# Moving the second stage of the later transforms to other places of a scheduled spectral mixture-of-experts kernel

## The chip, the cores and the metric

The kernel runs on one core of a Trainium2 chip. The metric is the time of one execution on the device in microseconds; the median of several runs counts.

## The reference

For each of 8 batches of 3072 tokens with 256 channels, the reference takes a real FFT along the tokens, multiplies by a complex filter, transforms back, and sends the result through two feed-forward layers:

```python
Y = np.fft.rfft(x, axis=1) * (filt_r + 1j * filt_i)
x = np.fft.irfft(Y, n=3072, axis=1)
xk = mu_k * x + (1 - mu_k) * x_prev
xr = mu_r * x + (1 - mu_r) * x_prev
v = np.maximum(xk @ w_k, 0) ** 2 @ w_v
x = sigmoid(xr @ w_r) * v
h = max(x @ w1, x @ w2, x @ w3)
out = h @ w_out
```

`x_prev` is `x` one token earlier. `w_k` is 256 x 1024, `w_v` 1024 x 256, `w_r` 256 x 256, `w1` to `w3` are 256 x 768, `w_out` is 768 x 256.

## The kernel before, in words

**Work.** A batch is one transform, and its 3072 tokens make 8 chunks of 384. Chunks are numbered through, 64 in all, and two of them make a pair. `kv(i)` (line 1367) is the first layer of chunk i: `r_mm`, then eight f-steps, each with six matmuls of `k_mm` (1204) and, from the fourth f-step on, six of `v_mm` (1217) for the f-step three back; the last three `v_mm` and `x2` are a tail that `mixed` (1457) sets between the units of what follows. `combos` (1236) makes sums of a pair's results. `second(p)` (1398) is the second layer of pair p: nine blocks of seven products (`block`, 1264), block k = 3 fq + j for weight j of the three and feature group fq; the last three products of a block run beside the next block. `out` (1311) takes the maximum over j, and at j = 2 splits it into two parts (`hh`, on ACT and POOL). `o_mm` (1335) multiplies these by `w_out`; it becomes due at k = 3, 6 and 9, with two calls to a block from k = 4 on, and what is left goes into the `kv` that follows. One `po` bank serves two calls of `o_mm` and stays open over all three groups. The main loop runs kv(2p+2), second(p), kv(2p+3) for one p after the other.

**The transform** (`fft`, 816) of a later batch runs inside this work, in pieces that hang at places: `put(place, fn)` (1465) files a piece, and `at_place` (1363) issues it when the loop comes to ("kv", i, f) or ("second", p, k). The first stage is 17 `a_step`s; their results go to DRAM (`s1a`, `s1b`; ACT copies them out of PSUM as `ao` and issues the write). The second stage has six steps u = 0 to 5. `b_load(u)` (894) loads matrices (`wbc`), the first stage's rows (`xb`) and two filter tiles (`filt`), five DMAs on SP's queue; `b_load(0)` is issued by the last `a_step`, `b_load(u+1)` by step u. `b_mm(u)` (908) multiplies into two PSUM banks (`pb`). `b_filt(u, z)` (914) multiplies bank z by the complex filter: ACT's two multiplications by a sign into `v`, DVE's three multiplications into `filt`, then POOL. `c_mm(u)` (933) transforms back from the two `yz` tiles into two banks (`pc`), one place later; `c_out` (939) copies them out on ACT (`co`) and writes them to `s2`, from which `y_load` (1151) and `y_mm` (1164) make the chunks. PSUM has eight banks, all under one tag (`pm`).

Transform b (1 to 7) is laid out at lines 1468 to 1489. For b from 2 on, with i = 8(b-1) and p = 4(b-1)-1, the last `a_step` is at ("kv", i+1, 7), and the second stage's seven places start at ("kv", i+2, 1), which comes right after kv(i+1).

**The order.** All calls after the opening are recorded by `Order` (220). PE's order is the order of the calls. For ACT, DVE, POOL and SP `play` (489) simulates the program with a cost for each instruction (`cost`, 292): `takes_ns` until its result is there, `holds` until its engine is free. Each engine takes, of the instructions that are ready, the one that is due first (`plan`, 329; `run`, 340). Calls are then issued in the order of the simulated starts. `use` (252) notes what an instruction has to wait for: here, writes before reads, and reads before writes. The waits in the program itself are set afterwards, from the issued order.

Of the kernel before, what the change touches and what calls it, by code (L numbers as in the profile page):

```python
# [32 lines left out]
NU4 = NG // 4  # L33
# [186 lines left out]
class Order:  # L220
# [31 lines left out]
    def use(self, o, ap, write):  # L252
        if isinstance(ap, Ref):
            name, dram = ap.tile.name, ap.tile.space == "DRAM"
        else:
            name, dram = ap.tensor.name, ap.space == bass.MemoryType.DRAM
        t = self.tiles.get(name)
        if t is not None:
            if not t.users and not t.early and t.order is not None:
                o.takes.append(t)  # L260
            if t not in o.takes and t.order is not None:
                o.needs.append(t.name)
            t.users.append(o.k)
        lo, hi, p0, p1 = self.box(ap)
        kept = []
        for e in self.seen.get(name, ()):
            k, w, a, b, c, d = e
            meet = a < hi and lo < b and c < p1 and p0 < d
            both = o.engine == "PE" and self.calls[k].engine == "PE" if k < o.k else True
            if meet and not both and (w or write) and not (dram and write):  # L270
                o.before[k] = True
            if not (write and not dram and lo <= a and b <= hi and p0 <= c and d <= p1):
                kept.append(e)
        kept.append((o.k, write, lo, hi, p0, p1))
        self.seen[name] = kept
# [16 lines left out]
    def cost(self, o, out, ins, k):  # L292
        n = int(np.prod(out.shape[1:]))
        psum = any(isinstance(v, Ref) and v.tile.space == "PSUM" for v in ins)
        e = o.engine
        o.shared = False
        o.quarter = False
        if "dma" in o.what:
            o.kind = "dma"
            o.holds = self.ISSUE[e]  # L300
            o.bytes = 4 * int(np.prod(out.shape))
            o.takes_ns = 0
            return
        o.kind = "op"
        if e == "PE":
            if k.get("tile_position") is not None:
                o.quarter = True
                o.holds, o.takes_ns = n // 2, 595
            elif k["lhsT"].dtype == F32R:
                o.holds = 4 + n * 0.4455 - (2 if n == 384 else 0)  # L310
                o.takes_ns = o.holds + 163
            else:
                o.holds = max(212, 8 + n * 1.667)
                o.takes_ns = o.holds + 165
        elif e == "ACT":
            o.takes_ns = 186 + n * 0.8 if psum else 175 + n * 0.89
            if n < 256:
                o.takes_ns = 330
        elif e == "DVE":
            both = len([v for v in ins if np.prod(v.shape[1:]) > 1]) > 1  # L320
            o.takes_ns = 150 + n * 1.065 if psum or both else 65 + n * 0.7
            o.shared = not psum
        else:
            o.takes_ns = 190 + n * 2.16 if len(ins) > 1 else 200 + n * 1.96
            o.shared = True
        if e != "PE":
            o.holds = o.takes_ns - self.OVERLAP[e]

    def plan(self, times):
        t, last = {}, 0.0  # L330
# [283 lines left out]
def tile_spectral_moe(ctx: ExitStack, tc, x, xr, xz, filt, ones, wa, wa1, wi, wbc, wb1, wc1, filt1, filt0, mu, w_k, w_v, w_r, w1, w2, w3, w_out, out):  # L614
    nc = tc.nc
# [42 lines left out]
    sg_s = cpool.tile([NK, 1], F32, name="sg_s")  # L658
# [157 lines left out]
    def fft(b):  # L816
# [48 lines left out]
        def quarters(o, of, whole=False):  # L865

            for k in range(1 if whole else 2):
                for y in (1, 0):
                    for x in range(2):
                        w, d = of(y, x, k)  # L870
                        to = o[y][x * H : x * H + H] if whole else o[y][x * H : x * H + H, k]
                        mm(to, w, d, k == 0, True, True, (y * H, x * H))
# [35 lines left out]
        def b_mm(u):  # L908
            w, f, t = st.pop(("b", u))
            p = [ps.tile([NK, 2, C], F32, tag="pm", name="pb") for _ in range(2)]  # L910
            quarters(p, lambda y, x, k: (w[y * H : y * H + H, 0, x, k], t[y * H : y * H + H, 2 * x + k]))
            st["f", u] = w, f, p, []

        def b_filt(u, z):
            w, f, p, y = st["f", u]
            fr, fi, q = f[z][:, 0], f[z][:, 1], p[z]
            v = fp.tile([NK, 2, C], F32, tag="flo", name="v", bufs=3)
            a, e = slice(0, NM), slice(NM, H)
            lo, hi = slice(H, H + NM), slice(H + NM, NK)
            nc.scalar.mul(v[lo], q[hi], sg_s[hi])  # L920
            nc.scalar.mul(v[hi], q[lo], sg_s[lo])
            nc.vector.scalar_tensor_tensor(fi[a], q[e], -1.0, fi[a], ALU.mult, ALU.mult)
            nc.vector.tensor_tensor(fi[e], q[a], fi[e], ALU.mult)
            nc.vector.tensor_tensor(fr, q, fr, ALU.mult)
            nc.gpsimd.tensor_tensor(fi[H:], v[H:], fi[H:], ALU.mult)
            yz = fp.tile([NK, 2, C], F32, tag="fin", name="yz")
            nc.gpsimd.tensor_tensor(yz, fr, fi, ALU.add)
            y.append(yz)
            if z:
                del st["f", u]  # L930
                st["c", u] = w, y

        def c_mm(u):
            w, t = st.pop(("c", u))
            p = [ps.tile([NK, 2, C], F32, tag="pm", name="pc") for _ in range(2)]
            quarters(p, lambda y, x, k: (w[y * H : y * H + H, 1, x, k], t[x][y * H : y * H + H, k]))
            st["o", u] = p

        def c_out(u, y):
            p = st["o", u][y]  # L940
            o = fp.tile([NK, 2, C], F32, tag="fo", name="co")
            nc.scalar.copy(o, p)
            g = 4 * u + 2 * y
            nc.scalar.dma_start(s2.rearrange("h m r g c -> (h m r) g c")[:, g : g + 2, :], o)

        def bc_step(u):
            if u < NU4:
                b_mm(u)
            if u:
                c_mm(u - 1)  # L950
            if u + 1 < NU4:
                b_load(u + 1)
            for z in range(2):
                if u < NU4:
                    b_filt(u, z)
            for z in range(2):
                if u:
                    c_out(u - 1, z)

        return a_step, bc_step  # L960

    def fft_first(pp, jobs, more):

# [182 lines left out]
    nc = order.nc  # L1146
# [301 lines left out]
    for _ in range(8):  # L1448

        p = ps.tile([P, NT], F32, tag="pm", name="pz")  # L1450
# [12 lines left out]
    steps = {}  # L1463

    def put(place, *fns):
        plan.setdefault(place, []).extend(fns)

    def transform(b):
        a_step, bc_step = fft(b)
        places, counts, bc = steps[b]  # L1470
        u = 0
        for place, n in zip(places, counts):
            for _ in range(n):
                put(place, lambda u=u: a_step(u))
                u += 1
        for u, place in enumerate(bc):
            put(place, lambda u=u: bc_step(u))

    for b in range(1, B):
        i, p = NCH * (b - 1), NCH // 2 * (b - 1) - 1  # L1480
        if b == 1:
            places = [("second", 0, k) for k in range(9)]
            bc = [("kv", 4, 1), ("kv", 4, 6), ("second", 1, 3), ("kv", 5, 7), ("kv", 6, 3), ("second", 2, 1), ("second", 2, 5)]
            counts = [2] * 8 + [1]
        else:
            places = [("kv", i, f) for f in (0, 2, 4, 6)] + [("second", p, k) for k in (4, 5, 6, 7, 8)] + [("kv", i + 1, f) for f in range(8)]
            bc = [("kv", i + 2, 1), ("second", p + 1, 3), ("kv", i + 3, 2), ("kv", i + 3, 7), ("kv", i + 4, 3), ("second", p + 2, 3), ("kv", i + 5, 3)]
            counts = [1] * 17
        steps[b] = places, counts, bc

    units = list(kv0)
    tail = []
    for i in (1, 2, 3):
        u, t = kv(i)
# [3 lines left out]
        tail = t  # L1498
    before2 = len(units)
    units.append(lambda: transform(1))  # L1500
    s, left = second(0)
    units += mixed(tail, s, 2)
    cm = lambda p: [lambda: combos(p)]
    tail = cm(1)
    for p in range(1, NPAIR):
        i = 2 * p + 2
        if i < NTOT:
# [3 lines left out]
            u, t = kv(i, left if p == 1 else ())  # L1511
# [5 lines left out]
        if i + 1 < NTOT:  # L1517
            end = i + 2 == NTOT
            u, t = kv(i + 1, () if end else left)
# [63 lines left out]
```

## Time and profile before

| | us |
|---|---|
| median of 3 runs | 3172.13 |
| lowest and highest | 3170.17, 3172.26 |
| profiled execution | 3172.82 |
| its span | 3171.1 |
| PE busy in it | 3066.8 (97%) |
| DVE, ACT, POOL busy | 1927.7, 1904.8, 1671.8 |

The span runs from the first profiled instruction to the last. Busy time is the union of an engine's instructions; matmuls are pipelined, so a busy PE is not one at its peak. A wait is the idle time of an engine before an instruction, booked on what came last.

### The profile page before, as it was taken

To read this page: it belongs to the slowest core of one execution; us is meant where nothing else is said; L and a number is where in the kernel's file an instruction comes from. 1 tells how busy PE (TensorE), PEld (TensorE's weight loads), DVE (VectorE), ACT (ScalarE), POOL (GpSimd) and SP (SyncE) were. 2 spreads that over 40 slices of the span, in tenths; PEclk is the share of its full clock that TensorE was granted. 3 is DMA by queue.
4 is the path that set the end of the run, shared out by engine and by line. 5 is a ranking of instruction groups with operands and counts; after the bars stand their busy time and mean duration, and the time that the engine had idled before them with its cause. 6 is when DMAs were issued, how large, how long until landed. Compare 5 with 4: busy or idle time off the path is not lost.

```text
span 3171.1 us, 56339 instructions
## 1 busy us (share of the span) xinstructions
PE 3066.8 (97%) x19816; PEld 2929.2 (92%) x19816; DVE 1927.7 (61%) x3061; ACT 1904.8 (60%) x3901; POOL 1671.8 (53%) x1416
## 2 busy tenths in 40 slices
PE   8899999999999999999999999999999999999998
PEld 5898999889998899899998999989999899999998
DVE  6886566566556665466655666556666565555554
ACT  6556656565655655566555665656555566555554
POOL 5435654575545655456445655457544465454543
PEclk9899999999999999999999999999999999999999
DMA  7788577766577765767656776576766765555554
GB/s 239 225 297 270 187 246 227 226 215 222 162 234 214 252 203 169 221 211 254 196 183 202 233 227 214 183 220 218 229 194 213 230 203 158 169 168 163 165 167 121
DMA packets 385192, 660.22 MB, mean 208 GB/s; under 512 B 41472, under 2 KB 150176, under 8 KB 384624
## 3 DMA queue, kind: packets, MB, share of 16 engines
q1 hardware_dynamic: 319584, 581.94, 59.5%
q10 hardware_dynamic: 64720, 72.52, 6.6%
q8 instruction: 159, 2.61, 0.4%
q0 software_dynamic: 608, 2.16, 0.2%
q14 instruction: 121, 0.99, 0.1%
HBM read 573.75 MB, written 82.71 MB: 207 GB/s over the span
## 4 chain that ended last, share of the span: by engine, by line
PE 87%; DMA 4%; ACT 3%; DVE 3%; POOL 2%; issue 1%; ACTq 0%; SPq 0%; POOLq 0%; DVEq 0%
PE pb L241 20%; PE pk L241 16%; PE pv L241 15%; PE po L241 12%; PE pe L241 9%; PE pa L241 6%; PE pr L241 4%; PE py L241 4%; ACT v L241 1%; DVE filt L241 1%; POOL hh L241 1%; PE ps L241 1%; DMA xb<-s1a 1%; DMA wci<-in_wc 1%; PE pc L241 1%
## 5 line engine op out<-in xcount | busy, mean ns | idle before, releaser
L241 POOL TENSOR_TENSOR hh<-m,hh 128x384 fp32r<-128x384 f32 x384 | 435.4, 1152 | 747.2 <-ACT hh L241 667.8
L241 PE MATMUL pb<-x,ws 128*128 128x384 f32 x3456 | 751.5, 339 | 23.0 <-ACT pa L241 17.1
L241 POOL TENSOR_TENSOR klo<-kr,khi 128x384 fp32r<-128x384 f32 x492 | 537.7, 1101 | 343.7 <-ACT khi L241 311.5
L241 PEld LDWEIGHTS pb<-x,ws 128*128 128x128 f32 x3456 | 600.2, 188 | 57.1 <-ACT pa L241 30.4
L241 DVE SCALAR_TENSOR_TENSOR kr<-pk,kr 128x384 f32<-128x384 f32 x512 | 281.9, 553 | 412.8 <-ACT kr L241 404.3
L241 PE MATMUL pv<-khi,ws 128*128 128x384 f32 x2048 | 525.7, 337 | 2.4 <-DVE filt L241 2.4
L241 PE MATMUL po<-wo_hi,hh 128*128 128x256 f32 x2304 | 500.4, 282 | 13.2 <-POOL hh L241 12.7
L241 PEld LDWEIGHTS po<-wo_hi,hh 128*128 128x128 f32 x2304 | 391.3, 189 | 16.2 <-POOL hh L241 15.5
L241 PE MATMUL pe<-x,ws 128*128 128x384 f32 x1728 | 395.2, 336 | 1.9 <-ACT ao L241 1.9
L241 ACT ACTIVATE kr<-pk 128x384 f32<-128x384 f32 x512 | 251.1, 490 | 207.2 <-PE pk L241 121.7
L241 PEld LDWEIGHTS pv<-khi,ws 128*128 128x128 f32 x2048 | 366.9, 189 | 8.7 <-DMA xb<-s1a 4.5
L241 PE MATMUL pk<-xh,wk_hi 128*128 128x384 f32 x1024 | 352.5, 344 | 5.5 <-DVE kr L241 2.9
L241 PE MATMUL pv<-klo,ws 128*128 128x384 f32 x1024 | 344.5, 336 | 1.4 <-POOL klo L241 1.4
L241 PE MATMUL pk<-xl,wk_hi 128*128 128x384 f32 x1024 | 344.6, 337 | 0.1
L241 PE MATMUL pk<-xh,wk_lo 128*128 128x384 f32 x1024 | 344.2, 336 | 0.0
L241 ACT CAST khi<-kr 128x384 fp32r<-128x384 f32 x512 | 261.3, 513 | 131.6 <-DVE kr L241 113.3
L241 POOL TENSOR_TENSOR xl<-xm,xh 128x768 fp32r<-128x768 f32 x126 | 239.7, 1916 | 185.7 <-ACT xh L241 183.2
L241 PE MATMUL po<-wo_lo,hh 128*128 128x256 f32 x1152 | 324.2, 281 | 0.0
L241 ACT CAST hh<-m 128x384 fp32r<-128x384 f32 x384 | 187.9, 514 | 195.4 <-DVE m L241 193.5
L241 DVE TENSOR_TENSOR m<-sc,m 128x384 f32<-128x384 f32 x384 | 297.4, 775 | 5.8
L241 PEld LDWEIGHTS pe<-x,ws 128*128 128x128 f32 x1728 | 295.8, 188 | 5.1 <-ACT ao L241 4.4
L241 ACT COPY u<-pb 128x384 f32<-128x384 f32 x288 | 138.1, 479 | 175.5 <-PE pb L241 173.3
(135 smaller groups left out, 5537.8 us busy)
## 6 DMA issues: line engine op xcount, KB each, us to landing
ws<-wud SPq DMA_DIRECT2D x864, 256.0 KB, 3.3
ws<-wvd SPq DMA_DIRECT2D x512, 256.0 KB, 3.1
filt<-in_filt SPq DMA_DIRECT2D x84, 512.0 KB, 4.7
ws<-wud SPq DMA_DIRECT2D x288, 128.0 KB, 3.3
xz<-in_xz SPq DMA_DIRECT2D x56, 512.0 KB, 5.8
cin<-s SPq DMA_DIRECT2D x128, 192.0 KB, 3.2
out_dram<-osb ACTq DMA_DIRECT2D x192, 128.0 KB, 3.1
xr<-in_xr SPq DMA_DIRECT2D x56, 384.0 KB, 5.0
```

The lines of the kernel that those rows point to most:

```text
L241: o = SimpleNamespace(engine=engine, call=lambda: call(*map(real, a), **{n: real(v) for n, v in k.items()}), what=call.__name__, k=len(sel ...
```

## The change

Four things change. (1) For transforms 2 to 7 the seven places of the second stage are others: a new function `spread` gives them. `bc_step` is parted into `b_step` and `c_step`; `c_step(u)` still hangs at the place of `b_step(u+1)`, and is now issued ahead of it. Transform 1 keeps its places. (2) In `b_filt` the second half (z = 1) issues ACT's two multiplications after DVE's three, the first half before them, as up to now. (3) The costs of ACT and DVE instructions are changed by some per cent, the sign multiplications get a cost of their own, and `holds` is longer for outputs on fewer than 128 partitions and for outputs in PSUM. (4) `use` makes a read of a PSUM tile wait, in the simulated order, for earlier reads of the same tile by another engine.

```diff
--- before.py
+++ after.py
@@ -263,9 +263,12 @@
             t.users.append(o.k)
         lo, hi, p0, p1 = self.box(ap)
         kept = []
+        psum = isinstance(ap, Ref) and ap.tile.space == "PSUM"
         for e in self.seen.get(name, ()):
             k, w, a, b, c, d = e
             meet = a < hi and lo < b and c < p1 and p0 < d
+            if not (w or write) and psum and k < o.k and self.calls[k].engine != o.engine:
+                o.before[k] = True
             both = o.engine == "PE" and self.calls[k].engine == "PE" if k < o.k else True
             if meet and not both and (w or write) and not (dram and write):
                 o.before[k] = True
@@ -313,18 +316,23 @@
                 o.holds = max(212, 8 + n * 1.667)
                 o.takes_ns = o.holds + 165
         elif e == "ACT":
-            o.takes_ns = 186 + n * 0.8 if psum else 175 + n * 0.89
+            o.takes_ns = 176 + n * 0.8 if psum else 175 + n * 0.88
             if n < 256:
-                o.takes_ns = 330
+                o.takes_ns = 342
+            if o.what == "mul":
+                o.takes_ns = 681 if psum else 614
         elif e == "DVE":
             both = len([v for v in ins if np.prod(v.shape[1:]) > 1]) > 1
-            o.takes_ns = 150 + n * 1.065 if psum or both else 65 + n * 0.7
+            o.takes_ns = 147 + n * 1.065 if psum or both else 65 + n * 0.7
             o.shared = not psum
         else:
             o.takes_ns = 190 + n * 2.16 if len(ins) > 1 else 200 + n * 1.96
             o.shared = True
         if e != "PE":
-            o.holds = o.takes_ns - self.OVERLAP[e]
+            part = out.shape[0] < 128
+            o.holds = o.takes_ns - self.OVERLAP[e] if not part else o.takes_ns + 40
+            if isinstance(out, Ref) and out.tile.space == "PSUM":
+                o.holds = o.takes_ns + 20
 
     def plan(self, times):
         t, last = {}, 0.0
@@ -917,11 +925,17 @@
             v = fp.tile([NK, 2, C], F32, tag="flo", name="v", bufs=3)
             a, e = slice(0, NM), slice(NM, H)
             lo, hi = slice(H, H + NM), slice(H + NM, NK)
-            nc.scalar.mul(v[lo], q[hi], sg_s[hi])
-            nc.scalar.mul(v[hi], q[lo], sg_s[lo])
+            def swap():
+                nc.scalar.mul(v[lo], q[hi], sg_s[hi])
+                nc.scalar.mul(v[hi], q[lo], sg_s[lo])
+
+            if not z:
+                swap()
             nc.vector.scalar_tensor_tensor(fi[a], q[e], -1.0, fi[a], ALU.mult, ALU.mult)
             nc.vector.tensor_tensor(fi[e], q[a], fi[e], ALU.mult)
             nc.vector.tensor_tensor(fr, q, fr, ALU.mult)
+            if z:
+                swap()
             nc.gpsimd.tensor_tensor(fi[H:], v[H:], fi[H:], ALU.mult)
             yz = fp.tile([NK, 2, C], F32, tag="fin", name="yz")
             nc.gpsimd.tensor_tensor(yz, fr, fi, ALU.add)
@@ -943,21 +957,19 @@
             g = 4 * u + 2 * y
             nc.scalar.dma_start(s2.rearrange("h m r g c -> (h m r) g c")[:, g : g + 2, :], o)
 
-        def bc_step(u):
-            if u < NU4:
-                b_mm(u)
-            if u:
-                c_mm(u - 1)
+        def b_step(u):
+            b_mm(u)
             if u + 1 < NU4:
                 b_load(u + 1)
             for z in range(2):
-                if u < NU4:
-                    b_filt(u, z)
+                b_filt(u, z)
+
+        def c_step(u):
+            c_mm(u)
             for z in range(2):
-                if u:
-                    c_out(u - 1, z)
-
-        return a_step, bc_step
+                c_out(u, z)
+
+        return a_step, b_step, c_step
 
     def fft_first(pp, jobs, more):
 
@@ -1466,27 +1478,33 @@
         plan.setdefault(place, []).extend(fns)
 
     def transform(b):
-        a_step, bc_step = fft(b)
-        places, counts, bc = steps[b]
+        a_step, b_step, c_step = fft(b)
+        places, counts, bp, cp = steps[b]
         u = 0
         for place, n in zip(places, counts):
             for _ in range(n):
                 put(place, lambda u=u: a_step(u))
                 u += 1
-        for u, place in enumerate(bc):
-            put(place, lambda u=u: bc_step(u))
+        for u in range(NU4):
+            put(bp[u], lambda u=u: b_step(u))
+            put(cp[u], lambda u=u: c_step(u))
+
+    def spread(i, p):
+        bc = [("kv", i + 2, 7), ("second", p + 1, 5), ("kv", i + 3, 1), ("kv", i + 3, 6), ("kv", i + 4, 3), ("second", p + 2, 4), ("kv", i + 5, 2)]
+        return bc[:-1], bc[1:]
 
     for b in range(1, B):
         i, p = NCH * (b - 1), NCH // 2 * (b - 1) - 1
         if b == 1:
             places = [("second", 0, k) for k in range(9)]
             bc = [("kv", 4, 1), ("kv", 4, 6), ("second", 1, 3), ("kv", 5, 7), ("kv", 6, 3), ("second", 2, 1), ("second", 2, 5)]
+            bp, cp = bc[:-1], bc[1:]
             counts = [2] * 8 + [1]
         else:
             places = [("kv", i, f) for f in (0, 2, 4, 6)] + [("second", p, k) for k in (4, 5, 6, 7, 8)] + [("kv", i + 1, f) for f in range(8)]
-            bc = [("kv", i + 2, 1), ("second", p + 1, 3), ("kv", i + 3, 2), ("kv", i + 3, 7), ("kv", i + 4, 3), ("second", p + 2, 3), ("kv", i + 5, 3)]
+            bp, cp = spread(i, p)
             counts = [1] * 17
-        steps[b] = places, counts, bc
+        steps[b] = places, counts, bp, cp
 
     units = list(kv0)
     tail = []
```

## Rows read from the trace of the kernel before

**Rows 1.** The page: busy us, share of the span and instructions of each engine.

```profile
PE 3066.8 (97%) x19816; PEld 2929.2 (92%) x19816; DVE 1927.7 (61%) x3061; ACT 1904.8 (60%) x3901; POOL 1671.8 (53%) x1416
```

**Rows 2.** PE's waits from 560 to 2640 us: us in total, times, longest us.

```profile
PE pb L241 <- DMA xb<-s1a: 30.3, 6, 5.9
PE pb L241 <- ACT pa L241: 12.5, 11, 1.5
PE po L241 <- POOL hh L241: 10.3, 12, 0.9
PE pk L241 <- DVE kr L241: 2.7, 6, 0.5
PE pv L241 <- DVE filt L241: 2.4, 6, 0.4
PE pb L241 <- DMA xb<-s1b: 0.8, 1, 0.8
PE pb L241 <- ACT u L241: 0.5, 3, 0.2
```

**Rows 3.** The chain of waits, 1326 to 1342 us: start us, us, what.

```profile
1331.11 3.56 DMA s1a<-ao
...
1335.32 4.41 DMA xb<-s1a
...
1339.86 2.10 PE pb L241 x16
```

**Rows 4.** Windows after the six stops (first, last, sum): busy us, then PEclk, DMA share, GB/s.

```profile
573.00:577.30 4.30, 4.19 (x23) 3.38 (x24) 1.45 (x3) 2.02 (x3) 0.56 (x1) 0.50 0.84 188
...
2488.70:2492.20 3.50, 3.50 (x21) 2.74 (x22) 0.80 (x2) 1.36 (x2) 0.00 (x0) 0.51 0.84 199
sum 24.60, PE 24.45 PEld 19.75 DVE 8.15 ACT 10.98 POOL 2.94; mean PE 4.07 PEld 3.29 DVE 1.36 ACT 1.83 POOL 0.49
```

**Rows 5.** Timeline of PE, 1333 to 1348 us: start us, us, instruction, count.

```profile
1344.29 0.52 PE L241 MATMUL pk<-xl,wk_hi 128*128 128x384 f32 x1
1344.61 0.52 PE L241 MATMUL pk<-xh,wk_lo 128*128 128x384 f32 x1
...
1346.53 0.33 PE L241 MATMUL pk<-xh,wk_lo 128*128 128x384 f32 x1
1346.70 0.51 PE L241 MATMUL pv<-khi,ws 128*128 128x384 f32 x2
...
1347.74 0.34 PE L241 MATMUL pk<-xh,wk_hi 128*128 128x384 f32 x1
```

**Rows 6.** PE's waits from 320 to 560 us, the largest.

```profile
PE pb L241 <- DMA ws<-wud: 1.8, 1, 1.8
```

**Rows 7.** Timeline of all engines around ("second", p+2, 3), 1083 to 1097 us, with [idle before].

```profile
1083.31 1.09 PE L241 MATMUL pb<-xb,wbc 64*64 64x256 f32 x16
...
1085.92 0.68 DVE L241 TENSOR_TENSOR filt<-pb,filt 32x512 f32<-32x512 f32 x1 [0.75 <-ACT v L241]
...
1086.63 1.38 ACT L241 ACTIVATE v<-pb,sg_s 32x512 f32<-32x512 f32 x2 [0.75 <-DVE filt L241]
...
1088.04 0.46 ACT L241 COPY pa<-pb 128x384 f32<-128x384 f32 x1
...
1088.56 0.79 PE L241 MATMUL pb<-x,ws 128*128 128x384 f32 x3 [1.53 <-ACT pa L241]
...
1094.45 0.68 DVE L241 TENSOR_TENSOR filt<-pb,filt 128x512 f32<-128x512 f32 x1
...
1095.39 0.39 PE L241 MATMUL po<-wo_hi,hh 128*128 128x256 f32 x1 [0.86 <-POOL hh L241]
```

**Rows 8.** Timeline of PE behind ("kv", i+3, 2), 1030 to 1040 us.

```profile
1036.36 0.59 PE L241 MATMUL pv<-khi,ws 128*128 128x384 f32 x2 [0.40 <-DVE filt L241]
...
1037.57 0.44 PE L241 MATMUL pk<-xh,wk_hi 128*128 128x384 f32 x1 [0.45 <-DVE kr L241]
```

**Rows 9.** Window of rows 7: busy us of PE, PEld, DVE, ACT, POOL, PEclk, DMA share, GB/s.

```profile
1083.00:1097.00 14.00, 11.46 (x86) 9.61 (x85) 10.52 (x19) 9.08 (x19) 9.29 (x8) 1.00 0.76 251
```

## The prediction

> **What bounds the kernel now.** I read the busy shares first: TensorE (PE) is busy 97% of the span and every other engine is far below [rows 1], so only what PE waits for, or what slows its matmuls, can move the end. Then I read PE's waits in the stretch that holds transforms 2 to 7, the ones whose places move [rows 2]. Their sum there is 59.5 us, and the largest item, 30.3 us in six pieces, is the first second-stage matmul of each transform waiting for its own load `xb`. The chain of waits around one of them shows why [rows 3]: the write of the first stage's last rows takes 3.56 us, the load that reads them back 4.41 us, and PE starts `pb` as soon as the load has landed. The order asks for `xb` two f-steps after the first stage ends, and a write and a read of HBM do not fit in there.
>
> The windows behind those six stops [rows 4] show a second cost: the granted clock is 0.50 to 0.53, the 1.2 GHz level, after PE has stood still for five or six microseconds. There, two matmuls of 384 columns start 0.32 us apart, and 0.17 us once the clock is back [rows 5]. The other waits of [rows 2] are short and belong to the later places: ACT `pa` and POOL `hh` in the two places in `second`, DVE `filt` and `kr` in the first place of `kv` after it.
>
> **The change part by part.** No matmul, vector operation or DMA is added or removed, so this is a sum of waits.
>
> *First place, six f-steps later.* One f-step issues six matmuls for `k_mm`, and from the third on six for `v_mm`; six take 1.04 us, from 1346.70 to 1347.74 [rows 5]. From ("kv", i+2, 1) to ("kv", i+2, 7) there are six `k_mm`, five `v_mm` and the last `v_mm` of the tail: 12 x 1.04 = 12.5 us. The longest wait of the six is 5.9 us [rows 2], so 6.6 us of cover remain, which a slower write or load would have to eat first. I take all six waits as gone: 30.3 us. A wait is counted from the end of the matmul before it, but back-to-back matmuls overlap (0.33 us long, started 0.17 us apart [rows 5]), so each removed wait brings 0.16 us more: 1.0 us. Bounds: 31.3 and 0. With the step move the five loads that `b_load(1)` puts on SP's queue and both filters' work. SP's loads of streamed weights run eight pieces ahead; the one case where PE did wait for such a piece cost 1.8 us [rows 6], so six transforms could lose at most 10 us by it. I take 0, because in transforms 2 to 7 no such wait appears though the same loads already pass there [rows 2].
>
> *The clock behind these stops.* The six low windows add up to 24.6 us [rows 4]. At half rate they hold the work of 12.3 us, so 12 us come back if no stop of that length takes their place. Bounds: 12 and 0. The Trainium skill, in "TensorE: Matmul & The Clock Gate" (Part 1), advises against fitting the ramp, since it is under 1% of a typical span; by that advice the 12 us would be left out and the forecast would read 3120 us. The rows have the clock at half for these windows, so they decide.
>
> *Places in* `second`, *from k = 3 to 5 and from 3 to 4.* What happens at k = 3 is in the timeline [rows 7]. ACT and DVE read the same `pb` banks in turns: DVE `filt` waits 0.75 us for ACT `v`, ACT `v` 0.75 us for DVE `filt`. ACT's copy `pa`, which PE needs next, stands in ACT's queue behind two such multiplications and starts at 1088.04; PE loses 1.53 us. Later the same filter work delays `hh`, which the first `o_mm` needs in the block after; PE loses 0.86 us. k = 3 is the one block where the block before ends a group (j = 2, four `hh` splits) and `o_mm` wants them at once in k = 4. At k = 5 the next `o_mm` of a new group is two blocks away, at k = 4 the `hh` that is due has been split already. So I take the `hh` waits as gone: 10.3 us, and 12 x 0.16 = 1.9 us, in all 12.2. The `pa` waits (12.5 + 0.8 us booked on `xb<-s1b`, and 1.9 us for 12 overlaps, 15.2 in all) have another cause, a 0.68 us multiplication ahead of a copy on ACT, and that can happen in any block. The new order knows that the two engines take turns at a bank, and the alternation of the second filter half lets DVE start one half while ACT does the other, so the ping-pong should shrink; I take half, 7.6 us. Bounds: all 15.2, and none.
>
> *Places in* `kv`. ("kv", i+3, 2) becomes 1, which puts one `k_mm` and one `o_mm` more between the step and the first `v_mm` that wants two banks. The waits are 2.4 us for DVE `filt`, which holds a bank, and 2.7 us for `kr`, queued behind it, in twelve pieces [rows 2, 8], with overlaps 7.0 us. But `y_mm` now follows the step instead of preceding it and asks for two banks and for ACT. I take half, 3.5 us. Bounds: 7.0 and, if `y_mm` waits as long as `v_mm` did, 0. The other three places move by at most one step and show no wait now.
>
> *c before b on PE, the alternation, the costs.* In one place PE now runs `c_mm(u-1)` ahead of `b_mm(u)`: the same 32 matmuls, 0. It lets ACT empty the two `pc` banks while PE works on `pb`. The alternation alone moves two 0.68 us operations per half on ACT behind DVE's; nothing on PE's path waits for them unless a bank is short: 0. The new costs and the read-after-read rule reorder all queues. Where PE has no wait, there is slack and I take 0; for new short waits at the twelve places in `second` I subtract 3 us, a quarter of a microsecond each (estimate: less than half of one 0.68 us multiplication), with 0 and -18 us (each place as bad as the 1.53 us of [rows 7]) as bounds. The opening and transform 1, whose places stay, I take as 0, with 4 us either way (estimate: two waits like that of [rows 6]).
>
> **The sum.** 31.3 + 12 + 12.2 + 7.6 + 3.5 - 3 = 63.6 us. The profiled execution took 3172.82 us, 1.7 us beyond its span of 3171.1; its forecast is 3109. The median of the three runs lies 0.7 us lower: **3108 us**. A change under 0.2%, some 6 us, could not be told from none.
>
> **Rivals.** (1) *The filter's waits move with it.* The `xb` waits and the clock come back, but the 34.5 us of short waits (28.7 and 36 overlaps) stay at the new places: 3172.1 - 43.3 = 3129 us. For it: ACT's 0.68 us multiplications stay as they are, and the new rule serialises every two reads of one PSUM tile by two engines. The Trainium skill ("PSUM — Partial Sum Buffer", PSUM bank collisions raise a hardware error) keeps two engines apart per bank and 32-partition quadrant only, which would make part of these turns unnecessary; [rows 7] show the waits between 32-partition pieces all the same, since the program waits by tile. Against it: the `hh` wait needs k = 3. (2) *Everything goes*, all 34.5 us: 31.3 + 12 + 34.5 = 78 us, 3094 us. (3) *The chain only moves.* ACT's copies, the write and the load are ordered by when they are due; due 12.5 us later, they could be put behind other work by as much, and PE would still wait about 5 us. Then only the 23.3 - 3 of the places come: 3152 us. Against it: an operation that is ready goes as soon as its queue is free, and ACT is busy only 60% [rows 1]. (4) *Slower: banks run out at k = 5.* One `po` bank is open there and none at k = 3; with two of `pc`, two of `pb`, the running block's and the late block's, eight may not do. The filter keeps its `pb` banks from 1083.31 until 1095.13 [rows 7], 11.8 us; if PE has to wait for them after some 4 us of other matmuls, that is 8 us at 12 places, 94 us, and at half clock afterwards some 2 us each [rows 4], 24 us more: 3172 + 118 - 43 = 3247 us. It decides from 43/12 = 3.6 us a place on. Against it: `pc` is emptied first now, and `kv`'s last two places, with `pv` open, have no wait today [rows 2].
>
> The skill's same clock page (A second HAM failure mode: psum-queue depth-cycling) has short stops between matmul groups lower the clock too; what is left of the waits would then cost twice. [Rows 9] are against it here: 14 us with those stops in them, granted clock 1.00.
>
> **How the numbers follow.** Forecast, 3098 to 3120: 0.52. Rival 1 with its neighbourhood to 3140: 0.22. Rival 2, 3086 to 3098: 0.14. Rival 3: 0.04. No effect because losses elsewhere cancel it: 0.02. Rival 4: 0.06. The first three hold 0.88, so 3086 to 3140 would be more than wanted, but the bounds of the parts overlap, and I keep 3088 as the lower and 3138 as the upper end. Faster 0.92, same 0.02, slower 0.06.
>
> **What would show it.** Right: no `pb` waiting for `xb<-s1a`, granted clock 1.00 from 560 us on, the `po` waits for `hh` gone in that stretch, `pa` waits about halved, PE's busy share near 98%. Wrong: a `pb`, `pv` or `py` that waits several microseconds for DVE `filt` or ACT `co` (banks), a wait for `ws` (loads displaced), or the sum of [rows 2] staying above 35 us.

## The result, and the profile after

The changed kernel takes 3087.74 us (median of four, 3085.93 to 3090.7) against 3172.2 us for the one before on the same chip: a ratio of 0.9732, interval 0.9716 to 0.9749. It is faster, as forecast, by 84.5 us where 64 were forecast, and lies 0.3 us below the lower end of the range (3088). The profiled executions differ by 86.9 us in span (3171.1 and 3084.2).

The page of the changed kernel: busy time by engine, and the granted clock in 40 slices (9 is 90% or more).

```profile
PE 3036.0 (98%) x19816; PEld 2919.1 (95%) x19816; DVE 1938.4 (63%) x3061; ACT 1906.1 (62%) x3901; POOL 1668.6 (54%) x1416
...
PEclk9899999999999999999999999999999999999999
```

PE's waits of the changed kernel from 550 to 2590 us, the stretch of transforms 2 to 7, answer to [rows 2]: us in total, times, longest us.

```profile
PE pk L241 <- DVE kr L241: 3.7, 6, 0.7
PE pb L241 <- DMA ws<-wud: 3.2, 6, 0.9
PE pb L241 <- ACT pa L241: 2.1, 5, 0.4
```

45 waits of 59.5 us have become 17 of 9.0 us. Neither `xb` nor `hh` is waited for, and no window of half clock is left between 250 us and the end of the stretch, where [rows 4] had 24.6 us of it.

To see where the time came from, I set marks at the same matmul in both traces: the first `pr` of chunk 4 (transform 1's second stage begins), of chunk 10 (transform 2's begins) and of chunk 54 (transform 7's is over). From the timeline of PE, start first. Before:

```profile
268.10 0.33 PE L241 MATMUL pr<-xh,wr_hi 128*128 128x384 f32 x1
...
561.42 0.44 PE L241 MATMUL pr<-xh,wr_hi 128*128 128x384 f32 x1
...
2677.10 0.33 PE L241 MATMUL pr<-xh,wr_hi 128*128 128x384 f32 x1
```

After:

```profile
267.03 0.33 PE L241 MATMUL pr<-xh,wr_hi 128*128 128x384 f32 x1
...
552.09 0.44 PE L241 MATMUL pr<-xh,wr_hi 128*128 128x384 f32 x1
...
2592.53 0.33 PE L241 MATMUL pr<-xh,wr_hi 128*128 128x384 f32 x1
```

| stretch | before, us | after, us | gain, us | forecast, us |
|---|---|---|---|---|
| up to chunk 4 | 268.1 | 267.0 | 1.1 | 0 |
| transform 1's second stage, transform 2's first | 293.3 | 285.1 | 8.3 | 0 |
| transforms 2 to 7 | 2115.7 | 2040.4 | 75.2 | 63.6 |
| the rest | 494.0 | 491.7 | 2.3 | 0 |

The first place of transform 4, for instance, has its load in time. The SP queue's row of the changed kernel for the two halves of that load, and the matmul that uses it:

```profile
1300.59 1.16 SPq L241 DMA_DIRECT2D xb<-s1a  x2
```

```profile
1313.59 1.09 PE L241 MATMUL pb<-xb,wbc 64*64 64x256 f32 x16
```

The second half is issued at 1301.2 and lands 4.7 us later, at 1305.9, which is 7.7 us before PE needs it. Over the six transforms this margin is 6.8 to 8.1 us; the prediction had put the cover at 6.6 us against the worst case.

At the second place, ("second", p+1, 5), the engines no longer take turns in the way of [rows 7]. Timeline of PE, ACT and DVE of the changed kernel, 1336 to 1350 us:

```profile
1336.05 1.09 PE L241 MATMUL pc<-yz,wbc 64*64 64x256 f32 x16
1336.97 1.04 PE L241 MATMUL pb<-xb,wbc 64*64 64x256 f32 x16
1337.24 1.07 ACT L241 COPY co<-pc 128x512 f32<-128x512 f32 x2 [1.31 <-PE pc L241]
...
1338.57 0.68 PE L241 MATMUL pe<-x,ws 128*128 128x384 f32 x3
1338.74 0.68 DVE L241 TENSOR_TENSOR filt<-pb,filt 32x512 f32<-32x512 f32 x1
1338.77 0.46 ACT L241 COPY pa<-pb 128x384 f32<-128x384 f32 x1 [0.46 <-PE pb L241]
1339.09 1.20 PE L241 MATMUL pb<-x,ws 128*128 128x384 f32 x6
1339.26 1.38 ACT L241 ACTIVATE v<-pb,sg_s 32x512 f32<-32x512 f32 x2
```

ACT empties the two `pc` banks while PE works on `pb`; its copy `pa` stands ahead of the multiplications `v`, not behind them, and PE does not wait.

### The profile page after: what moved, and what is told of

Same layout as the page of the kernel before. It is cut to its first block, busy times and chain, and to the rows that moved or that the text cites. A ratio compares the mean times of both kernels' runs of the same rounds, so it can differ in the third digit from the quotient of the medians.

```text
span 3084.2 us, 56469 instructions
## 1 busy us (share of the span) xinstructions
PE 3036.0 (98%) x19816; PEld 2919.1 (95%) x19816; DVE 1938.4 (63%) x3061; ACT 1906.1 (62%) x3901; POOL 1668.6 (54%) x1416
## 4 chain that ended last, share of the span: by engine, by line
PE 92%; DMA 3%; ACT 2%; issue 1%; DVE 1%; POOL 1%; ACTq 0%; SPq 0%; POOLq 0%; DVEq 0%
PE pb L241 20%; PE pk L241 17%; PE pv L241 16%; PE po L241 12%; PE pe L241 9%; PE pa L241 6%; PE pr L241 4%; PE py L241 4%; DMA ws<-wud 1%; PE pc L241 1%; PE ps L241 1%; DMA s<-co 1%; ACT v L241 0%; PE pc L650 0%; DMA s1a<-ao 0%
## 5 line engine op out<-in xcount | busy, mean ns | idle before, releaser
L241 PE MATMUL pb<-x,ws 128*128 128x384 f32 x3456 | 743.3, 338 | 9.3 <-ACT pa L241 4.0
L241 PEld LDWEIGHTS pb<-x,ws 128*128 128x128 f32 x3456 | 601.3, 188 | 37.0 <-issue 14.6
L241 DVE TENSOR_TENSOR m<-sc,m 128x384 f32<-128x384 f32 x384 | 290.2, 758 | 5.5
L241 DVE SCALAR_TENSOR_TENSOR xm<-yt,nmu_s,xm 128x384 f32<-128x384 f32 x256 | 215.9, 868 | 84.8 <-ACT xm L241 76.9
```

Source lines behind the costliest of these rows:

```text
L241: o = SimpleNamespace(engine=engine, call=lambda: call(*map(real, a), **{n: real(v) for n, v in k.items()}), what=call.__name__, k=len(sel ...
```

## The experiments

All times are medians; a ratio is to the kernel before, measured beside it on the same chip. Stretches are those of the table above, between the same marks. In the diffs, a line with a minus is the kernel that the experiment starts from.

**The places.** First the changed kernel with its old places, the old kernel with the new ones, and the old kernel with the first place alone moved.

```diff
@@ e1_old_places, from the changed kernel (e2_places_only is the reverse, from the kernel before)
-        bc = [("kv", i + 2, 7), ("second", p + 1, 5), ("kv", i + 3, 1), ("kv", i + 3, 6), ("kv", i + 4, 3), ("second", p + 2, 4), ("kv", i + 5, 2)]
+        bc = [("kv", i + 2, 1), ("second", p + 1, 3), ("kv", i + 3, 2), ("kv", i + 3, 7), ("kv", i + 4, 3), ("second", p + 2, 3), ("kv", i + 5, 3)]
@@ e3_first_only, from the kernel before
-            bc = [("kv", i + 2, 1), ("second", p + 1, 3),
+            bc = [("kv", i + 2, 7), ("second", p + 1, 3),
```

> The changed kernel with the seven old places for transforms 2 to 7; costs, read rule, alternation and c ahead of b stay. Theory A (the order won the short waits and transform 1, the places won only the xb waits and the clock behind them): the xb waits of some 30 us and the half clock come back, 43 us, and nothing else: 3131 us, short waits in transforms 2 to 7 below 12 us. Rival B (as the prediction had it: the hh waits need another place): the hh waits of 12 us and half the pa waits come back as well: 3150 us. Rival C (the places won all in transforms 2 to 7): 3162 us, with 29 us of short waits back.

Measured: 3131.7 us, ratio 0.9869 (0.9852 to 0.9885). Theory A fits to the microsecond, and B and C fall. PE's waits of e1, 554 to 2638 us:

```profile
PE pb L241 <- DMA xb<-s1a: 28.2, 6, 5.1
PE pr L241 <- ACT co L241: 5.3, 6, 0.9
PE pb L241 <- ACT pa L241: 2.2, 5, 0.4
PE pb L241 <- ACT v L241: 1.2, 1, 1.2
```

The `xb` waits are back and the `hh` waits are not, though the step is at k = 3 again. The new order removes them without the new place.

> The kernel before with the new places alone; b_mm ahead of c_mm, old costs, no read rule, no alternation. Theory A: 43 us gone, the 29 us of short waits stay at the new places, with hh replaced by other waits: 3129 us. Rival B: hh waits gone, pa waits not: 3117 us. Rival C: 3097 us, transform 1 and the opening as before. If the load xb is still waited for, it is above 3150 us.

Measured: 3127.2 us, 0.9852 (0.9837 to 0.9867): near A's 3129. But the short waits did not stay; others took their place. PE's waits of e2, 559 to 2630 us:

```profile
PE pe L241 <- DVE filt L241: 13.7, 6, 2.3
PE py L241 <- DVE filt L241: 4.2, 6, 1.0
PE pb L241 <- ACT pa L241: 1.9, 6, 0.4
PE pb L241 <- ACT u L241: 1.8, 6, 0.3
PE pb L241 <- DMA ws<-wud: 0.7, 2, 0.4
PE pe L241 <- DVE sc L241: 0.6, 1, 0.6
PE pr L241 <- DVE filt L241: 0.3, 1, 0.3
```

Here the `hh` waits are gone with the old order: the new places remove them too, without it.

But at ("second", p+1, 5) PE stands 2.3 us in each transform until DVE gives a bank of the filter back: rival 4 of the prediction, in a small form, with the old order.

> The kernel before with only the first of the seven places moved, from ('kv', i+2, 1) to ('kv', i+2, 7). All theories: the xb waits (31 us) and the clock behind them (12 us) go, 3129 us, granted clock 1.00 in transforms 2 to 7. If the write and load of the rows only move with their due time: 3165 to 3172 us.

Measured: 3133.4 us, 0.9874 (0.986 to 0.9889), 40 us below the 3173.7 us of the kernel before beside it; 37.9 us of it lie in transforms 2 to 7. The `xb` waits go, and PE's other waits are nearly those of [rows 2]: `hh` 10.3 us in 12, `kr` 2.7 us in 6, `filt` 2.4 us in 6, but `pa` 14.5 us in 15. That is the first two terms of the sum measured alone: 40 us for 43.3.

**The parts of the order.** Then the changed kernel without the read rule, without the alternation, with `b_mm` ahead of `c_mm`, and with the old costs; and the rule alone.

```diff
@@ e4_no_read_rule (e8_rule_only puts these two lines, and the one that sets `psum`, into the kernel before)
-            if not (w or write) and psum and k < o.k and self.calls[k].engine != o.engine:
-                o.before[k] = True
@@ e5_no_alternation
-            if not z:
-                swap()
+            swap()
...
-            if z:
-                swap()
@@ e6_b_before_c
-            put(bp[u], lambda u=u: b_step(u))
-            put(cp[u], lambda u=u: c_step(u))
+            put(bp[u], lambda u=u: b_step(u))
+            if u:
+                put(cp[u - 1], lambda u=u: c_step(u - 1))
+        put(cp[NU4 - 1], lambda: c_step(NU4 - 1))
@@ e7_old_costs and e15_old_costs_again: the ACT, DVE and holds lines of cost() as before
```

> The changed kernel without the rule that makes a read of a PSUM tile wait, in the simulated order, for another engine's earlier read. Theory A with the rule as the main part of the order: ACT and DVE take turns again inside one bank, pa waits of some 15 us in transforms 2 to 7 and some 4 us in transform 1 return: 3107 us. Rival (the costs or the alternation do it, the rule little): 3088 to 3092 us.

Measured: 3116.2 us, 0.9816 (0.9802 to 0.9831), 28 us above the changed kernel's 3087.7. The rule matters more than A's price for it, but not through the `pa` waits. The largest of PE's waits of e4, 559 to 2617 us:

```profile
PE pk L241 <- DVE kr L241: 5.5, 6, 1.3
PE pc L241 <- POOL yz L241: 4.8, 6, 0.9
PE pb L241 <- ACT v L241: 3.5, 6, 0.6
PE pb L241 <- ACT pa L241: 2.2, 5, 0.4
```

PE waits for the filter's banks and its results at several places, 19.0 us in all where the changed kernel waits 9.0; that a mis-ordered filter ends late is my reading of it. The waits are not the whole price: in the profiled execution (3110.5 us) transforms 2 to 7 take 2058.5 us here and 2040.4 with the rule, and transform 1's stretch 291.8 us here and 285.1 with it.

> The changed kernel with ACT's two multiplications ahead of DVE's three in both halves of the filter. Theory A (the read rule makes the gain, the alternation shortens each filter by some 1.4 us that PE rarely waits for): 3088 to 3094 us. Rival (rule and alternation only pay together, since with the rule alone DVE stands while ACT does its half): about 3105 to 3116 us, as without the rule, with PE waiting for DVE filt.

Measured: 3093.1 us, 0.9755 (0.9741 to 0.977). As A says: the alternation is worth some 5 us, though the two intervals overlap. None of it shows in transforms 2 to 7 (2040.7 us against 2040.4); transform 1's stretch has 3.9 us of it (289.0 against 285.1).

> The changed kernel with b_mm ahead of c_mm in a place, as before. Theory A (the order of the two on PE is worth nothing by itself): 3086 to 3091 us. Rival (c first is what gives the pc banks back in time at the new places): waits for ACT co or DVE filt of 1 to 2 us a place, 3097 to 3110 us.

Measured: 3116.8 us, 0.9824 (0.981 to 0.984), 29 us above the changed kernel. A falls; the rival fits, and its upper end is too low. The largest of PE's waits of e6, 555 to 2623 us:

```profile
PE pe L241 <- DVE filt L241: 14.5, 5, 2.9
PE pb L241 <- ACT pa L241: 3.5, 11, 0.4
PE pe L241 <- ACT co L241: 3.1, 1, 3.1
```

What stands in the way is in the timeline of e6 at the second place, 972 to 985 us:

```profile
972.11 1.09 PE L241 MATMUL pb<-xb,wbc 64*64 64x256 f32 x16
973.02 1.04 PE L241 MATMUL pc<-yz,wbc 64*64 64x256 f32 x16
...
975.35 1.37 ACT L241 ACTIVATE v<-pb,sg_s 32x512 f32<-32x512 f32 x2
976.04 1.38 DVE L241 TENSOR_TENSOR filt<-pb,filt 32x512 f32<-32x512 f32 x2
976.75 1.07 ACT L241 COPY co<-pc 128x512 f32<-128x512 f32 x2
...
977.68 1.30 PE L241 MATMUL pe<-x,ws 128*128 128x384 f32 x3 [2.90 <-DVE filt L241]
```

With `b_mm` first, ACT finds the filter's work ready before `pc`, so it copies `pc` out only at 976.75, and the last read of `pb` ends at 977.42. Until then two `pb`, two `pc`, one `po`, the late block's `pb` and the running block's `pb` and `pa` hold all eight banks (counted from the program), and `pe` would be the ninth. With `c_mm` first the copies start right behind it, at 1337.24 in the rows of the changed kernel. The clock adds to the price: all six stops have half clock behind them, 20.5 us of it in all, which at half rate is some 10 us (estimate) beside the 17.6 us of the stops. The window behind one of them (us of the window, busy of PE, PEld, DVE, ACT and POOL, PEclk, DMA share, GB/s):

```profile
977.70:981.20 3.50, 3.50 (x12) 3.50 (x13) 1.65 (x3) 0.38 (x2) 2.88 (x3) 0.55 0.69 227
```

> The changed kernel with the old costs of ACT and DVE instructions. Theory A (the rule is the main part, the costs differ by some per cent only): 3086 to 3093 us. Rival (the sign multiplications, planned 85 ns too short, make the order miss its starts): pa waits of 8 to 15 us return, 3098 to 3106 us.

Measured: 3083.2 us, 0.9724 (0.9708 to 0.974): below A's range, and far from the rival's. The new costs gain nothing.

> The kernel before with the read rule alone. Theory A (the rule is worth the same 28 us here as in the changed kernel): 3144 us, hh and pa waits mostly gone, the xb waits still there. Rival (the rule pays only with the alternation and the new costs): 3160 us or more. If all of the order's 42 us come from it: 3132 us.

Measured: 3155.5 us, 0.9946 (0.9931 to 0.996): 16 us, between A's 28 and the rival's 12 or less. The rule alone halves the `hh` waits (5.4 us in 12) and brings `pa` from 12.5 to 2.2 us. In transform 1's stretch it brings 293.3 us to 287.1, most of what the whole change gains there. The rule is worth 28 us in the changed kernel and 16 us alone; why less was not shown.

**Is it banks?** Then e6 with its second place where no `po` bank is open, and the changed kernel with it where two are.

```diff
@@ e9_b_first_k4, from e6: ("second", p + 1, 5) becomes ("second", p + 1, 4)
@@ e10_c_first_k6, from the changed kernel: ("second", p + 1, 5) becomes ("second", p + 1, 6)
@@ e11_rule_places_c_first: the changed kernel with the edits of e5 and e7
@@ e12_old_holds, from the changed kernel
-            part = out.shape[0] < 128
-            o.holds = o.takes_ns - self.OVERLAP[e] if not part else o.takes_ns + 40
-            if isinstance(out, Ref) and out.tile.space == "PSUM":
-                o.holds = o.takes_ns + 20
+            o.holds = o.takes_ns - self.OVERLAP[e]
```

> The changed kernel with b_mm ahead of c_mm (as e6) and the second place one block earlier, ('second', p+1, 4), where no po bank is open. Theory A (e6's waits of pe for DVE filt, 2.9 us each, come from a bank that po holds at k = 5): those waits and the half clock behind them go, 3088 to 3095 us. Rival (b ahead of c costs that at any place, since both pc and pb banks are taken for the whole filter): pe still waits 1 us or more for DVE filt, 3105 to 3120 us.

Measured: 3090.8 us, 0.9741 (0.9724 to 0.9758): A. With `b_mm` first, one block earlier, the `pe` waits are gone, and the kernel is within 3 us of the changed one. PE's waits of e9, 553 to 2595 us:

```profile
PE pb L241 <- ACT pa L241: 4.3, 15, 0.4
PE pb L241 <- DMA ws<-wud: 1.4, 4, 0.5
PE py L241 <- DVE kr L241: 1.1, 2, 0.7
```

> The changed kernel (c ahead of b) with the second place one block later, ('second', p+1, 6), where two po banks are open. Theory A (banks decide, and c first buys about one bank's worth): PE waits 1 to 3 us per transform for DVE filt or ACT co, some with half clock behind, 3097 to 3115 us. Rival (c first makes the place indifferent): 3085 to 3091 us. If the hh split of the group that ends at k = 5 is what suffers: po waits for hh of about 0.9 us each, 3094 us.

Measured: 3089.4 us, 0.9737 (0.9719 to 0.9754): A falls, the rival holds. With `c_mm` first two open `po` banks are no harm, nor does `hh` come late.

> The kernel before with three parts only: the new places, the read rule and c ahead of b; old costs, no alternation. Theory A (these three carry the gain; alternation 5 us, costs nothing): 3086 to 3095 us. Rival (one of the two small parts is needed once the other is missing): 3100 us or more.

Measured: 3092.2 us, 0.9744 (0.9724 to 0.9764): A. Places, rule and `c_mm` first make some 80 us of the 84. With the old costs, then, the alternation is worth some 6 to 9 us (e7, the same with it, has 3083.2 us and 0.9724), though the intervals overlap.

> The changed kernel with the new durations but the old rule for how long an instruction holds its engine. Theory A (the costs matter little either way): 3083 to 3090 us. If the longer holds are what makes e7 some 5 us better than the changed kernel: 3081 to 3084 us; if the durations: 3086 to 3091 us.

Measured: 3090.1 us, 0.9737 (0.972 to 0.9754). It does not reach e7's 3083, so by its own criterion the durations, not the holds, are what costs time; a single measurement with overlapping intervals is thin for that.

**What was still open:** whether `c_mm` first pays by itself, and whether the old costs are really better.

```diff
@@ e13_c_first_only, from the kernel before, in bc_step
+            if u:
+                c_mm(u - 1)
+                for z in range(2):
+                    c_out(u - 1, z)
             if u < NU4:
                 b_mm(u)
-            if u:
-                c_mm(u - 1)
...
```

> The kernel before with c_mm ahead of b_mm alone; old places, old costs, no read rule, no alternation. Theory A (c first is worth something only where banks are short, and at the old places none was waited for by more than 0.4 us): 3166 to 3174 us, hh and pa waits as before. Rival (c first pays anywhere, 20 us or more as e6 lost): 3150 us or less.

Measured: 3167.4 us, 0.9981 (0.9972 to 0.999): A by the time, not by the waits. From e13's waits, 560 to 2680 us:

```profile
PE pk L241 <- DVE filt L241: 11.0, 6, 1.8
PE pb L241 <- ACT u L241: 8.3, 11, 1.1
PE pb L241 <- ACT pa L241: 1.0, 2, 0.7
```

The `hh` waits of [rows 2] are gone here too, and the `pa` waits nearly, but much of it comes back at other places, and four of the six stops of 1.8 us for `filt` have half clock behind them. What in the old plan makes these waits was not shown.

> The changed kernel itself, to be compared with the same kernel with old costs on one chip: 3084 to 3092 us by either theory.

> The changed kernel with the old costs (as e7). If the new costs really lose time: 3081 to 3086 us, 3 to 6 us below the changed kernel of the same call. If e7 was a scatter of runs: within 2 us of it.

Measured: 3088.8 us for the changed kernel, 0.9738 (0.9724 to 0.9751), and **3081.6 us** for it with the old costs, 0.9714 (0.9701 to 0.9728). No run of one falls into the other's spread (3086.3 to 3092.0, and 3079.5 to 3083.6), though the intervals overlap by 0.0004. In transforms 2 to 7 e15 waits for next to nothing (550 to 2590 us):

```profile
PE pb L241 <- ACT pa L241: 2.0, 11, 0.2
PE pb L241 <- DMA ws<-wud: 0.5, 1, 0.5
```

This is the fastest version tried: the changed kernel with the cost lines taken back.

## Why the prediction was wrong in size

The forecast named the right large waits and came out too small. In the profiled executions the gain is 86.9 us where the sum has 63.6. Of the 23.3 us between them, the short waits and delays of transforms 2 to 7 make 9.8, the opening and transform 1 9.4, the rest of the program 2.3, and 1.8 stay open. Rival 2 (everything goes) had the measured time in its band of 3086 to 3098, but not for its reason alone: 9.0 us of waits stayed, and 11.7 us came from outside transforms 2 to 7.

**Right.** *The first place.* Forecast 31.3 us of `xb` waits: all six are gone, and e1 brings 28.2 us of them back. *The clock.* Forecast 12 us: no half clock is left, and e3, which moves that place alone, gains 40 us, more than the 31.3 us of the waits by themselves. The Trainium skill, in "TensorE: Matmul & The Clock Gate" (Part 1), puts the penalty of the warm-up ramp under 1% of a typical kernel span and advises against fitting a count of cold matmuls. The 12 us behind these stops are 0.4% of this span, which agrees with it, and yet a seventh of the gain. *Rival 1* (the short waits stay) falls with the 9.0 us that are left of them. *Rival 3* (the chain only moves) is excluded by the rows of the load, *rival 4* (slower) by the result, and its mechanism is real: see below.

**Wrong, though not in the total: the step "c before b on PE ... the same 32 matmuls, 0".** No matmul is added, and still the step is worth 29 us at the new places (e6). I had named what it does, that ACT can empty `pc` while PE works on `pb`, and then did not ask what the banks would do without it, though rival 4 counted them. What e6 and e2 show in its place: at k = 5 a stop of 2.3 to 3.1 us in each transform for a bank, and mostly half clock behind it. At k = 4 (e9) it is gone. The forecast is not too small because of this step: the sum had counted the new places as free of such stops, and at k = 5 they are so only with `c_mm` first.

**Half right: "the** `hh` **wait needs k = 3".** I gave 12.2 us to the place and half of the `pa` waits to the order. The place does remove the `hh` waits (e2), but it is not needed: e1 has the old place and no `hh` wait, and e13 has none either, with the old place and `c_mm` first alone; the read rule alone halves them (e8). How `c_mm` first does it was not shown. With the new order, the places' own share is the `xb` wait and the clock: the changed kernel and e1 differ by 44 us.

**Mis-sized: the short waits.** Forecast 20.3 us net (12.2 + 7.6 + 3.5 - 3) in transforms 2 to 7. The rows show 29.2 us of them before (59.5 without `xb`) and 9.0 after; with 0.16 us of overlap for each of 22 waits fewer that is 23.7 us. The step that failed most is the `pa` waits, "I take half, 7.6 us": 12.5 us in 11 waits became 2.1 in 5, nearly all of them. Against that stand `kr`, which stayed (2.7 and 3.7 us), and six waits for `ws`, 3.2 us, where the prediction took 0 for displaced loads. What the sum lacked besides is what no wait row holds. Outside half clock, start to start, 206 neighbouring matmuls in that stretch of the trace before were 0.06 to 0.14 us later than the median of their kind, 21 us in all, against 147 with 14.6 us after, 6.4 us less. In each trace 67 of them stand behind the 64x64 matmuls of a transform, at the same price. 39 before and 17 after are the second matmul behind a booked wait, 2.4 us of the difference; [rows 7] have one, where the three matmuls behind the wait take 0.79 us and three take 0.68 in the changed kernel's rows. What delays the others, 4.0 us of the difference, was not found. So the term is 30 us instead of 20.3, and with the forecast 43.3 us for `xb` and clock 73 of the 75.2 us are found; the rest stays open.

**Mis-sized: "the opening and transform 1, whose places stay, I take as 0, with 4 us either way".** It was 9.4 us. Of this, 1.1 us lies up to chunk 4 and is within the scatter of that mark (264.0 to 269.4 us in the traces of all runs). In transform 1's stretch the read rule does most of it: the rule alone gains 6.2 of the 8.3 us there (e8, 287.1 us), and without it the changed kernel loses 6.7 of them (e4, 291.8 us). A rule that reorders every filter can be worth something at all 42 steps, not just at those whose place moves, and I had charged the short waits only where places move.

**Rival 1's ground** was that the rule serialises too much. The Trainium skill, in "PSUM — Partial Sum Buffer" (PSUM bank collisions raise a hardware error), keeps two engines apart per bank and 32-partition quadrant, while the program here waits by tile. The runs decide about the plan, not about the chip: a plan that knows the program's waits is 28 us better than one that does not (e4). Whether finer waits would gain more was not tried.

**The costs** were forecast to be worth nothing, and lose some 5 to 7 us (e7, e15).

## What to carry to other kernels

When a schedule is written by a simulation, a wait that the program has and the simulation lacks can cost more than durations that are off by some per cent: here the read rule was worth 28 us, and the changed durations nothing. When a step is reordered without adding work, count the buffers that are held in both orders at the place where they are shortest; "the same instructions" says nothing on that. Parts of a change should be measured by taking each one away from the whole, and also alone: the rule cost 28 us when removed and gave 16 us alone, `c_mm` first 29 and 5. The 29 us hang on the place: with `b_mm` first, but the second place one block earlier, the kernel is within 3 us of the changed one (e9).

## What was not expected of the hardware

A stop of some 2 us can be enough for the lower clock, and need not be. In e2 PE stood 2.29 us at the second place of each of the six transforms, and behind five of them the clock records show a stretch at 0.50; in e6, with 2.9 or 3.1 us, all six have one. In e13 PE stood 1.8 us for `filt` once in each transform, and four of the six have one. Two of those windows (us of the window, busy of PE, PEld, DVE, ACT and POOL, PEclk, DMA share, GB/s):

```profile
1049.90:1053.30 3.40, 3.40 (x12) 3.40 (x12) 1.22 (x2) 2.09 (x5) 3.32 (x4) 0.51 0.45 158
1432.90:1436.30 3.40, 3.39 (x20) 3.40 (x21) 1.82 (x3) 2.71 (x6) 3.32 (x3) 1.00 0.54 187
```

Behind the five stops of 1.5 us in the kernel before, one of them in [rows 9], the clock had stayed at 1.00. In these traces the length of a stop alone does not decide.
